# Fewer filler products on TensorE ahead of the last weights of a spectral mixer

## Chip, cores and metric

The kernel runs on one core of a Trainium2 chip. The metric is device time in microseconds (us), the median over several executions. Times are compared with executions of the kernel before on the same chip in the same job, and where a comparison goes across jobs the text says so. The span of a profile (first to last instruction) is about 2.3 us shorter than the device time of the same execution.

TensorE is called PE below, VectorE DVE, ScalarE ACT, GpSimd POOL. PSUM is the memory in which PE's products are summed. A weight *lands* when the DMA transfer that loads it is complete. The *granted clock* is the share of PE's full clock that the profile records.

## The reference, cut to what matters

```python
attn = linear_attention(q, k, v)                  # 8 x 8 heads x 576 x 64, elu + 1 features
x = attn.transpose(0, 2, 1, 3).reshape(8, 576, 512)
X = np.fft.rfft(x, axis=1)                        # the first 64 modes are used
Yr = einsum('bmd,mde->bme', Xr, w_r) - einsum('bmd,mde->bme', Xi, w_i)
Yi = einsum('bmd,mde->bme', Xr, w_i) + einsum('bmd,mde->bme', Xi, w_r)
y = np.fft.irfft(Yr + 1j * Yi, n=576, axis=1)     # other modes are zero
u = x + y
out = u + np.maximum(u @ w_ch, 0.0)
```

Each of the 64 modes has two weights of 512 x 512, `w_r` and `w_i`. Together that is 128 loads which the kernel casts to bf16 while loading, and they fill most of the time (55.7% of the span on the chain of waits of the kernel before).

## The kernel before

The modes are computed in the order in which their weights land. Every mode is two groups of four concurrent products (`t = 1` with `wr`, `t = 0` with `wi`), an eviction from PSUM (by DVE for even modes, ACT for odd ones), and four small products that gather the result (`yt`). By the timeline of before such a group of four takes 0.47 us at full clock, where three fillers in a row, of as many columns each, take 0.82. The last mode, 63, is computed in a turned form, 16 columns wide, so that no eviction and gathering follow it: one copy puts it into `YT`. In the last four modes the kernel adds *fillers*: products whose result nobody reads, meant to keep PE's clock up. The code is shortened; comments stand for what is left out.

```python
def keep_warm(n):
    for _ in range(n):                         # 128 rows, 512 columns, result overwritten later
        pin(nc.tensor.matmul(last_ps[0], id16, wch16[:, 0, :]))

def mode_product(kk, ps, stage, yt_ps):
    wr, wi = w_get(kk)
    # ... st: the evicted mode; P: a PSUM bank
    for t, w in ((1, wr), (0, wi)):
        for dc in range(NDC):                  # NDC = 4 concurrent products, 32 columns of the array each
            mm = nc.tensor.matmul(P[0][dc * 32 : dc * 32 + 32, :], xt_cols(dc, t, kk), w[:, dc, :],
                                  start=(t == 1), stop=(t == 0), tile_position=(0, dc * 32))
        if t == 1 and kk >= NM - 4:
            keep_warm(6)                       # between wr and wi
    if NM - 4 <= kk < NM - 1:
        keep_warm(3)                           # during the eviction
    # ... evict P to st (DVE or ACT), four products yt <- pick_sb, st
    if NM - 4 <= kk < NM - 1:
        keep_warm(3)                           # before the next mode

def last_mode(ps):                             # kk = NM - 1 = 63
    wr, wi = w_get(kk)
    # ... product(t, w, dcs): for each dc four products of 16 columns into y_last
    product(1, wr, range(NDC))
    keep_warm(3)
    product(0, wi, range(3))                   # wi of mode 63 is loaded in two parts
    product(0, wi, range(3, NDC))
    nc.vector.tensor_copy(out=YT[:, :, kk, :], in_=y_last)
```

After the copy into `YT` come eight products `zl <- wch, YT` and four transposes `ypl`, two copies into `last`, and then the output stage: for 36 row tiles the inverse transform and the channel product are summed in PSUM (`acc`), rectified by ACT, added to `x` by DVE and stored.

Of the kernel before, what the change touches and what calls it, by code (L numbers as in the profile page):

```python
# [47 lines left out]
def kernel(  # L48
# [48 lines left out]
    def xt_cols(dc: int, t: int, kk: int):  # L97

        c0 = dc * XDC + t * B * NM + kk
        return xt_c[:, c0 : c0 + 31 * NM + 1 : NM]  # L100
# [231 lines left out]
    def w_get(kk: int):  # L332
        if kk not in w_in:
            w_in[kk] = [w_load(kk, half, wpool, "w", W_KEEP) for half in range(2)]
        return w_in.pop(kk)

    def keep_warm(n: int):

        for _ in range(n):
            pin(nc.tensor.matmul(last_ps[0], id16, wch16[:, 0, :]))  # L340

    def mode_product(kk: int, ps, stage, yt_ps):

        wr, wi = w_get(kk)
        st = stage.tile([128, D], F16, tag="ystage", bufs=2, name=f"ys{kk}")

        n_part = 1
        pw = D // n_part
        P = [
            ps.tile([128, D], F32, tag="P", bufs=2, name=f"P{kk}_{i}")[:, 0:pw] for i in range(n_part)  # L350
        ]
        for t, w in ((1, wr), (0, wi)):
            for i in range(n_part):
                for dc in range(NDC):
                    mm = nc.tensor.matmul(  # L355
                        P[i][dc * 32 : dc * 32 + 32, :], xt_cols(dc, t, kk),
                        w[:, dc, i * pw : i * pw + pw],
                        start=(t == 1), stop=(t == 0), tile_position=(0, dc * 32),
                    )
                    if kk >= NM - 4:  # L360
                        pin(mm)
            if t == 1 and kk >= NM - 4:
                keep_warm(6)
        if NM - 4 <= kk < NM - 1:
            keep_warm(3)
        for i in range(n_part):
            dst = st[:, i * pw : i * pw + pw]
            if (kk + i) % 2 == 0:
                nc.vector.tensor_copy(out=dst, in_=P[i])  # L369
            else:  # L370
                nc.scalar.copy(out=dst, in_=P[i])  # L371
        for ec in range(NDC):
            mm = nc.tensor.matmul(  # L373
                yt_ps[:, ec, kk % 8, :], st[:, ec * 128 : ec * 128 + 128], pick_sb
            )
            if kk >= NM - 4:
                pin(mm)
        if NM - 4 <= kk < NM - 1:
            keep_warm(3)

    def last_mode(ps):

        kk = NM - 1
        wr, wi = w_get(kk)
        y_last = ps.tile([128, NDC, 2 * B], F32, tag="P", bufs=2, name="y_last")

        def product(t, w, dcs):
            for dc in dcs:
                c0 = dc * XDC + t * B * NM + kk
                x = xt_c[:, c0 : c0 + (2 * B - 1) * NM + 1 : NM]  # L390
                for ec in range(NDC):
                    pin(
                        nc.tensor.matmul(
                            y_last[:, ec, :], w[:, dc, ec * 128 : ec * 128 + 128], x,
                            start=(t == 1 and dc == 0 and ec == 0), stop=(t == 0 and dc == NDC - 1),
                            skip_group_check=True,
                        )
                    )

        product(1, wr, range(NDC))  # L400
        keep_warm(3)
        product(0, wi, range(3))
        product(0, wi, range(3, NDC))
        nc.vector.tensor_copy(out=YT[:, :, kk, :], in_=y_last)
# [23 lines left out]
    def mode(kk: int):  # L428
        nonlocal yt_ps
        if kk % 8 == 0:  # L430
            yt_ps = psW.tile([128, NDC, 8, 2 * B], F32, tag="yt", bufs=1, name=f"yt{kk // 8}")
        if kk == NM - 1:
            last_mode(psW)
            return
        mode_product(kk, psW, ystage, yt_ps)
        if kk == NM - 2:
            nc.vector.tensor_copy(out=YT[:, :, NE : NM - 1, :], in_=yt_ps[:, :, 0 : NL - 1, :])
        elif kk % 8 == 7:
            nc.vector.tensor_copy(out=YT[:, :, kk - 7 : kk + 1, :], in_=yt_ps)
# [299 lines left out]
```

## Time and profile before

| | before |
|---|---|
| device time, median of 3 | 432.05 us (431.16 to 432.51) |
| span of the profile | 429.8 us |
| weights | stream at about 214 GB/s to about 390 us |
| last landing of a weight (DMA records) | 394.50 us |
| start of the last copy into `YT` | 395.68 us |
| from there to the end of the span | 34.1 us |

First the page's slices of the kernel before: PE's busy share and its granted clock, each in tenths, in 40 slices of 10.7 us.

```profile
PE   0358776887018776856886666778675758999993
PEclk9999666565558765566556678555658655999998
```

(The first 9s of the clock lie before the first record of it.) In most of the span PE alternates between half and full clock; only slices 34 to 38, counted from 0, from 365 us on, run at full clock throughout, and PE is busy in nearly all of that time.

Next the chain of waits of the kernel before, at its last modes. Columns are start, duration, engine and work.

```profile
...
386.66 1.40 PE zl L340 x6
388.06 0.40 PE P L355 x3
...
394.05 0.47 PE y_last L393 x16
394.52 0.65 PE zl L340 x3
395.17 0.49 PE y_last L393 x16
...
395.68 0.23 DVE YT L404
...
395.97 1.06 PE zl L674 x8
...
397.62 1.03 PE acc L549 x4
...
```

`zl L340` are the fillers: they stand on the chain itself. Nothing in this stretch waits for a DMA: between 382 and 396 us the view of PE's waits has one line (total in us, times, longest).

```profile
PE zl L674 <- DVE YT L404: 0.3, 1, 0.3
```

Now four stretches of the same profile that coincide with the 3.41 us steps of its clock records. Columns are the stretch, its length, the busy time of PE, PEld (weight loads), DVE, ACT and POOL with the number of instructions, the granted clock, the DMA share and GB/s.

```profile
384.69:388.10 3.41, 3.36 (x24) 1.20 (x22) 0.59 (x1) 0.00 (x0) 0.00 (x0) 1.00 1.05 211
388.10:391.52 3.42, 3.42 (x23) 1.27 (x24) 0.00 (x0) 0.58 (x1) 0.00 (x0) 1.00 0.92 179
391.52:394.93 3.41, 3.36 (x35) 1.56 (x34) 1.31 (x2) 0.00 (x0) 0.00 (x0) 1.00 0.26 47
394.93:398.34 3.41, 2.71 (x34) 1.97 (x32) 0.65 (x2) 1.26 (x3) 0.19 (x1) 1.00 0.00 0
```

PE is busy nearly all the time in the first three, for 2.71 of 3.41 us in the fourth, and the clock is 1.00 in all four. The output stage of the same kernel, in the same columns, is PE's as well: it is busy in every moment of 19.3 us.

```profile
402.70:422.00 19.30, 19.30 (x98) 8.91 (x98) 17.14 (x14) 15.53 (x30) 0.00 (x0) 1.00 0.91 364
```

### The profile page before, as it was taken

The page shows a single profiled execution, that of the slowest core. Times are in us where ns is not written, and L with a number is a line of the kernel's source. Part 1 is how long each engine was busy: PE and PEld are TensorE (multiplying, and loading weights), DVE is VectorE, ACT ScalarE, POOL GpSimd, SP SyncE. Part 2 cuts the span into 40 slices and gives each one's busy share as a digit, 9 for nine tenths or more (in the row PEclk, how much of TensorE's full clock was granted, in tenths as well). Part 3 has the DMA queues.
Part 4 walks back from the last instruction along what each step waited for, and adds up shares of the span by engine and source line. Part 5 has one row for each costly group of instructions (what it writes and reads, how often), then busy time and mean ns, then how long its engine had stood idle before and what let it go on. Part 6 is the DMA issues. An engine that isn't in the chain of part 4 may idle for free.

```text
span 429.8 us, 6238 instructions
## 1 busy us (share of the span) xinstructions
PE 296.9 (69%) x2551; PEld 154.8 (36%) x2551; DVE 181.9 (42%) x373; ACT 146.6 (34%) x227; POOL 91.5 (21%) x165
## 2 busy tenths in 40 slices
PE   0358776887018776856886666778675758999993
PEld 0346555664003332322232222322222324954441
DVE  1699998955004233233232322332323322211694
ACT  3687666631002222222222322122212222311782
POOL 4232223222102312121112221221211121110200
PEclk9999666565558765566556678555658655999998
DMA  8999999999999999999999999999999999995697
GB/s 148 207 208 209 209 210 210 211 214 215 222 211 214 215 213 214 214 214 214 213 213 214 214 213 214 213 214 214 213 213 214 214 214 214 214 213 97 239 369 296
DMA packets 35803, 92.38 MB, mean 215 GB/s; under 512 B 3136, under 2 KB 16448, under 8 KB 35776
## 3 DMA queue, kind: packets, MB, share of 16 engines
q0 software_dynamic: 32000, 82.00, 98.2%
q1 hardware_dynamic: 3776, 10.00, 6.1%
q8 instruction: 20, 0.33, 0.3%
q14 instruction: 7, 0.06, 0.0%
HBM read 164.07 MB, written 9.44 MB: 404 GB/s over the span
## 4 chain that ended last, share of the span: by engine, by line
DMA 67%; PE 17%; issue 7%; DVE 4%; ACT 2%; POOL 1%; DVEq 0%; POOLq 0%; ACTq 0%
DMA wi<-in_moe_w_i_dram 33%; DMA wr<-in_moe_w_r_dram 22%; DMA k<-in_k_dram 11%; PE acc L549 4%; PE P L355 3%; PE z L530 2%; PE zl L340 2%; PE acc L593 2%; PE eps L507 2%; PE yp L534 1%; DVE x L272 1%; ACT ke L187 1%; DVE k L194 0%; ACT qT L223 0%; POOL q L169 0%
## 5 line engine op out<-in xcount | busy, mean ns | idle before, releaser
L507 PE MATMUL eps<-wch,xTw 128*128 128x512 f16 x144 | 62.3, 582 | 3.4 <-DVE xTw L504 3.1
L515 ACT CAST E<-eps 128x512 f16<-128x512 f32 (+1 forms) x40 | 21.3, 543 | 122.7 <-PE eps L507 122.7
L115 POOL DMA_DIRECT2D wr<-in_moe_w_r_dram x64 | 34.0, 531 | 135.5 <-PE P L355 109.4
L355 PE MATMUL P<-wi,xt_c 128*32 128x512 bf16 x252 | 42.1, 565 | 27.3 <-DMA wi<-in_moe_w_i_dram 27.3
L355 PE MATMUL P<-wr,xt_c 128*32 128x512 bf16 x252 | 42.6, 582 | 22.9 <-DMA wr<-in_moe_w_r_dram 20.9
L115 POOL DMA_DIRECT2D wi<-in_moe_w_i_dram x65 | 34.5, 531 | 108.5 <-PE P L355 74.1
L355 PEld LDWEIGHTS <-xt_c 128*32 128x32 bf16 x504 | 24.3, 163 | 67.8 <-issue 38.7
L369 DVE CAST ys<-P 128x512 f16<-128x512 f32 x32 | 22.0, 688 | 59.7 <-PE P L355 59.7
L151 PEld LDWEIGHTS <-qT 64*128 64x128 f16 (+1 forms) x640 | 21.5, 126 | 56.8 <-issue 41.8
L371 ACT CAST ys<-P 128x512 f16<-128x512 f32 x31 | 18.1, 585 | 63.2 <-PE P L355 63.0
L373 PE MATMUL yt<-pick_sb,ys 128*128 128x16 f16 x252 | 16.8, 177 | 31.6 <-DMA pick_sb<-row_pick 20.4
L504 DVE COPY xTw<-xTp 128x512 f16<-128x512 f16 x36 | 15.2, 423 | 51.8 <-PE xTp L502 51.8
L373 PEld LDWEIGHTS <-ys 128*128 128x128 f16 x252 | 12.3, 105 | 51.1 <-issue 23.4
L151 PE MATMUL num<-kv,qT 64*128 64x65 f16 (+1 forms) x320 | 14.0, 230 | 22.6 <-ACT kv L247 20.1
L507 PEld LDWEIGHTS <-xTw 128*128 128x128 f16 x144 | 14.7, 124 | 33.7 <-issue 24.2
L492 DVE TENSOR_TENSOR x_main<-nw,rd 128x256 f32<-128x256 f32 x32 | 12.1, 419 | 33.8 <-PE nw L151 33.7
L187 ACT ACTIVATE qe<-q 128x1152 f16<-128x1152 f16 x16 | 17.7, 1155 | 22.9 <-DMA q<-in_q_dram 22.9
L216 PE MATMUL qTp<-id,qe 128*128 128x128 f16 x144 | 16.6, 310 | 12.1 <-DVE qe L200 11.7
L499 ACT CAST x16w<-x_main 128x512 f16<-128x512 f32 x32 | 19.8, 619 | 14.2 <-DVE x_main L492 14.2
L272 DVE TENSOR_TENSOR x<-num,rd 128x512 f16<-128x512 f32 x32 | 22.1, 691 | 1.1
L491 DVE RECIPROCAL rdw<-nw 128x4 f32<-128x4 f32 (+1 forms) x40 | 5.5, 170 | 38.3 <-PE nw L151 38.2
L502 PE MATMUL xTp<-id,x16w 128*128 128x128 f16 x144 | 19.4, 278 | 2.8 <-ACT x16w L499 2.4
(71 smaller groups left out, 413.7 us busy)
## 6 DMA issues: line engine op xcount, KB each, us to landing
wr<-in_moe_w_r_dram POOLq DMA_DIRECT2D x64, 512.0 KB, 18.6
wi<-in_moe_w_i_dram POOLq DMA_DIRECT2D x63, 512.0 KB, 18.6
out_dram<-x_main SPq DMA_DIRECT2D x14, 512.0 KB, 3.1
q<-in_q_dram POOLq DMA_DIRECT2D x8, 576.0 KB, 13.5
k<-in_k_dram POOLq DMA_DIRECT2D x8, 576.0 KB, 14.7
v<-in_v_dram POOLq DMA_DIRECT2D x8, 576.0 KB, 16.9
out_dram<-x_main SPq DMA_DIRECT2D x4, 256.0 KB, 3.4
out_dram<-x_tail SPq DMA_DIRECT2D x2, 512.0 KB, 3.4
```

Source lines behind the costliest of these rows:

```text
L115: tc.keep_in_program_order(nc.gpsimd.dma_start(out=w[:, dcs], in_=rows_of[:, dcs, :]))
L151: mm = nc.tensor.matmul(num[hpo][orow, c0 : c0 + 65], qT[rows, hpp, h2, cols], kv_sb[rows, hpp, h2, :])
L187: pin(nc.scalar.activation(out=ev[:, c], in_=heads(nm, b)[:, c], func=AF.Exp))
L272: nc.vector.tensor_tensor(out=dst.rearrange("p (o c d) -> p o c d", o=2, c=4), in0=nv[:, :, :, 0:64], in1=rden.unsqueeze(3).broadcast_to([ ...
L355: mm = nc.tensor.matmul(P[i][dc * 32 : dc * 32 + 32, :], xt_cols(dc, t, kk), w[:, dc, i * pw : i * pw + pw], start=(t == 1), stop=(t == 0) ...
L369: nc.vector.tensor_copy(out=dst, in_=P[i])
L371: nc.scalar.copy(out=dst, in_=P[i])
L373: mm = nc.tensor.matmul(yt_ps[:, ec, kk % 8, :], st[:, ec * 128 : ec * 128 + 128], pick_sb)
L499: nc.scalar.copy(out=x16, in_=x)
L502: nc.tensor.transpose(xT_ps[:, c, :], x16[:, c * 128 : c * 128 + 128], id16)
L507: nc.tensor.matmul(e_ps, xT[:, c, :], wch16[:, c, :], start=(c == 0), stop=(c == NDC - 1))
L515: nc.scalar.copy(out=dst, in_=e_ps[:, cols])
```

## The change

The intent was to take fillers away where they delay PE. There were 39; 20 are left. `FILL[kk]` gives the numbers between `wr` and `wi`, during the eviction, and before the next mode. The diff is shortened.

```diff
             if t == 1 and kk >= NM - 4:
-                keep_warm(6)
+                keep_warm(FILL[kk][0])
         if NM - 4 <= kk < NM - 1:
-            keep_warm(3)
+            keep_warm(FILL[kk][1])
 # ... eviction and yt products
         if NM - 4 <= kk < NM - 1:
-            keep_warm(3)
+            keep_warm(FILL[kk][2])
+
+    FILL = {60: (2, 1, 1), 61: (4, 2, 2), 62: (4, 2, 1), 63: (1, 0, 0)}
 # ... last_mode
         product(1, wr, range(NDC))
-        keep_warm(3)
+        keep_warm(FILL[kk][0])
         product(0, wi, range(3))
```

Nothing else changes its order on any engine. (The line numbers of later code move by two: L674 of before is L676 after.)

## The prediction

> **What bounds the kernel now.** Median 432.05 us; profiled span 429.8. The page's slices show DMA at 90% or more until slice 36 (weights, about 214 GB/s); the chain of waits is 67% DMA, but only up to 360 us. Then PE is behind (timeline): YZ rows to 379, two accumulators to 382.3, then modes 60 to 63 with 39 fillers to 395.7, all on the chain. From 397.6 to 422 PE is 95 to 100% busy at full clock (stretch table).
>
> **What the change removes.** Fillers go 12 to 4, 12 to 8, 12 to 7 and 3 to 1: 19 of 39, spaced 0.217 us, so 4.1 us of PE work on the chain. The rest keeps its order; the weight DMAs were all issued by 380.8, before the first filler, so they don't move.
>
> **How much is critical.** Landings before (DMA records): wr62 387.1, wi62 389.55, wr63 392.0, the two parts of wi63 393.85 and 394.5. PE used them at 390.06, 391.86, 393.89 and 395.01, so never waited, with 0.5 us of slack at the end. Laid out with before's durations (product 0.41, its end to yt about 0.8, yt 0.11):
> - wr61 at 384.9, wi61 386.3, wr62 388.1: PE-limited.
> - wi62 meets its landing (389.6); wr63 waits to 392.05; wi63 to 393.9, its last quarter to 394.55.
> - The last copy into YT starts near 395.05 in place of 395.68.
>
> So 0.6 (0.5 to 0.8) of 4.1 us is gained; the rest becomes PE waiting for DMA.
>
> **The clock.** [...] the trace's clock records agree (1.0 or 0.5, in steps of 3.41 us). I added up streamed columns per window, as a share of it. Full-clock windows up to about 0.38 were followed by half, from 0.38 by full; half-clock windows needed 0.66 or more to go up. Before, the last windows have 0.73 and more, and 0.59 at 394.9. In the changed kernel, windows starting between about 388.6 and 393.4 would have 0.13 to 0.35 (a y_last product streams 16 columns, a filler 512). That range is longer than a window, so whatever the phase one is too idle: chance of a drop 85% (estimate). Full clock returns after a dense window, at 397.8 to 401.2. Half clock from 395.1 to there costs 1.3 to 2.9 us; the PE-bound output stage can't win it back.
>
> Sum: -0.6, and +1.2 to +2.7 with a drop. Predicted 433.2 us, 8 in 10 between 430.8 and 435.0. Chances: faster by over 2% 0.01, within 2% 0.98, slower 0.01.
>
> **What the profile would show.**
> - 20 fillers (L340); landings unmoved within 0.5 us.
> - PE waits for DMA wr/wi between 389 and 394.6; the chain's DMA part ends at wi63's landing.
> - y_last's copy at 394.8 to 395.2.
> - Clock 0.5 for one or two windows within 392 to 401; zl products from YT at 0.4 us or more in place of 0.27. Once full again, the output stage takes before's time.
> - Last accumulation at 423 to 425 in place of 422.
>
> **What would make it wrong.** [...] If the tail re-warms at once, about even. If the clock falls already in modes 61 to 62, or re-warming takes longer, 435 or more. If landings move, so does the 0.6.

Two passages are cut out of it: a premise about what sets the clock, and a condition built on that premise. 432.05 - 0.6, and 1.2 to 2.7 more with a fall of the clock, is 432.7 to 434.2 us, and about 431.4 without a fall. "The clock" rests on the trace of before: its clock records (only 1.0 and 0.5, in steps of 3.41 us) and its products. The sums per window, their limits of 0.38 and 0.66, the moment at which full clock returns and the cost of 1.3 to 2.9 us are my estimates from that trace; how the sums are scaled stands below, above their table.

## The result, and the profile after

The changed kernel took 432.62 us (median of 4, 432.27 to 433.06) against 431.69 us of the kernel before (4 executions). The ratio is 1.002, with a 95% interval of 0.9999 to 1.0042. A repetition below (e1) shows that it is truly slower, by 0.43%.

The slices after, as above:

```profile
PE   0358677797028776777687677677787858976993
PEclk9999866655558866555856558556555568997998
```

PE's share in slices 35 and 36 (376 to 398 us) falls from 9 to 7 and 6 tenths, and in slice 36 the clock has a 7 where before had a 9. The chain of waits shows the same stretch:

```profile
...
378.14 15.67 DMA wi<-in_moe_w_i_dram
...
393.86 0.30 PE y_last L395 x4
...
394.19 0.24 DVE YT L406
...
394.47 1.90 PE zl L676 x8
...
396.97 1.77 PE acc L551 x4
...
```

The fillers have left the chain. In their place stands the load of the last weight, landed at 393.82; the last four products follow 0.04 us later and the copy into `YT` starts 0.37 us after the landing (before: 1.18 us after it). That is the gain. The loss comes next: the eight `zl` products take 1.90 us, not 1.06, and the four `acc` products 1.77 us, not 1.03, together 1.6 us more. The durations agree with the clock records: the median `zl` product takes 273 ns where they say full clock and 421 ns where they say half. Two lines from the view of the tile `zl` (shortest, median and longest duration in ns), the first of before, the second of after:

```profile
L674 PE MATMUL zl<-wch,YT x8: 272/273/283, 396.0 to 396.7; 128*128 128x256 f16 x8
```

```profile
L676 PE MATMUL zl<-wch,YT x8: 394/421/421, 394.5 to 395.9; 128*128 128x256 f16 x8
```

PE's waits in the changed kernel, from 380 us on (total, times, longest):

```profile
PE P L355 <- DMA wi<-in_moe_w_i_dram: 1.3, 2, 1.0
PE y_last L395 <- DMA wi<-in_moe_w_i_dram: 0.8, 1, 0.8
PE yt L373 <- DVE ys L369: 0.7, 2, 0.5
PE y_last L395 <- DMA wr<-in_moe_w_r_dram: 0.7, 1, 0.7
PE P L355 <- DMA wr<-in_moe_w_r_dram: 0.6, 1, 0.6
...
```

These are 3.4 us of waiting for weights (1.3 + 0.8 + 0.7 + 0.6), where the kernel before had none; the longest single wait is 1.04 us. The removed fillers were 4.1 us (19 at 0.217 us), so most of them turned into waits. And the stretches of the clock, in the columns used before:

```profile
384.86:388.28 3.42, 2.25 (x15) 0.83 (x15) 0.00 (x0) 0.27 (x1) 0.00 (x0) 1.00 1.05 211
388.28:391.69 3.41, 1.81 (x22) 0.79 (x22) 1.32 (x2) 0.00 (x0) 0.00 (x0) 1.00 0.93 180
391.69:395.10 3.41, 2.17 (x32) 1.27 (x29) 0.22 (x1) 0.00 (x0) 0.00 (x0) 0.50 0.18 33
395.10:398.51 3.41, 3.23 (x14) 1.71 (x13) 0.42 (x1) 1.87 (x4) 0.81 (x2) 0.50 0.00 0
402.70:422.00 19.30, 19.22 (x97) 8.90 (x96) 17.15 (x14) 15.53 (x31) 0.00 (x0) 1.00 0.92 367
```

A window in which PE was busy for 1.81 of 3.41 us was followed by half clock for two windows. From 398.5 on the clock is full again and the output stage is as before. What it lost in those windows it never wins back.

The sum over the whole tail is simple. In the kernel before, 34.1 us pass from the start of the copy into `YT` to the end of the span; in the changed kernel 35.8 us (430.0 - 394.19). The copy starts earlier, but 1.7 us more follow it.

### The profile page after: what moved, and what is told of

Read it like the earlier page. It is cut to its first block, busy times and chain, and to the rows that moved or that the text cites. A ratio compares the mean times of both kernels' runs of the same rounds, so it can differ in the third digit from the quotient of the medians.

```text
span 430.0 us, 6200 instructions
## 1 busy us (share of the span) xinstructions
PE 296.6 (69%) x2532; PEld 153.6 (36%) x2532; DVE 181.8 (42%) x373; ACT 146.8 (34%) x227; POOL 91.5 (21%) x165
## 4 chain that ended last, share of the span: by engine, by line
DMA 67%; PE 13%; issue 8%; DVE 8%; POOL 2%; ACT 1%; DVEq 0%; POOLq 0%; ACTq 0%
DMA wi<-in_moe_w_i_dram 37%; DMA wr<-in_moe_w_r_dram 22%; DMA k<-in_k_dram 7%; PE acc L551 4%; DVE x L272 3%; PE P L355 2%; PE z L532 2%; PE acc L595 2%; PE eps L509 1%; PE yp L536 1%; DVE qe L200 1%; DVE q L194 1%; DVE rd L269 1%; DVE k L194 1%; DVE ke L200 1%
## 5 line engine op out<-in xcount | busy, mean ns | idle before, releaser
L355 PE MATMUL P<-wi,xt_c 128*32 128x512 bf16 x252 | 43.1, 573 | 26.6 <-DMA wi<-in_moe_w_i_dram 26.5
L494 DVE TENSOR_TENSOR x_main<-nw,rd 128x256 f32<-128x256 f32 x32 | 12.1, 420 | 34.2 <-PE nw L151 34.2
```

Source lines behind the costliest of these rows:

```text
L355: mm = nc.tensor.matmul(P[i][dc * 32 : dc * 32 + 32, :], xt_cols(dc, t, kk), w[:, dc, i * pw : i * pw + pw], start=(t == 1), stop=(t == 0) ...
```

## The experiments

Theory A: the fillers were on PE's chain, but the landing of the last weight caps the gain at about 0.6 us; the idle time so made lets the clock fall, which costs 1 to 3 us. Rival B: the clock does not matter at the end; the fillers just became waits for DMA.

| run | median | before in the same job | ratio (95%) | copy into `YT` starts | from there to the end | clock after 384 us |
|---|---|---|---|---|---|---|
| e1 changed kernel again | 433.14 | 431.27 | 1.0043 (1.0028 to 1.0058) | 394.40 | 36.5 | half, 393.2 to 400.0 |
| e2 fillers in the waits | 430.85 | 431.27 | 0.9992 (0.9977 to 1.0007) | 394.26 | 34.0 | full |
| e3 fillers of 32 rows | 438.77 | 431.27 | 1.0176 (1.0154 to 1.0197) | 400.81 | 35.5 | half, 387.2 to 404.3 |
| e4 no fillers | 432.51 | 431.27 | 1.0027 (1.0014 to 1.0039) | 394.12 | 36.1 | half, 386.3 to 400.0 |
| e5 before, no last load | 431.81 | 431.85 | 0.9994 (0.9977 to 1.0011) | 394.85 | 34.0 | full |
| e6 changed, no last load | 428.88 | 431.85 | 0.9935 (0.9918 to 0.9952) | 392.13 | 34.3 | full |
| e7 more fillers in mode 63 alone | 431.26 | 431.85 | 0.9984 (0.9968 to 1.0000) | 394.95 | 34.2 | full |
| e8 as e6, more fillers in mode 62 | 428.63 | 431.85 | 0.9932 (0.9914 to 0.9950) | 392.05 | 34.1 | full |
| e9 e2 again | 430.85 | 431.54 | 0.9982 (0.9970 to 0.9995) | 395.26 | 33.9 | full |
| e10 e7 again | 430.97 | 431.54 | 0.9984 (0.9970 to 0.9997) | 394.18 | 34.1 | full |

The last three columns are of the one profiled execution of each. "Full" is to the end of the last accumulation or beyond it. The column "from there to the end" is the span less the copy's start: 33.9 to 34.3 us wherever the clock stays full, 35.5 to 36.5 wherever it does not.

### e1: the changed kernel again

No edit. 

> The changed kernel once more, to get its difference clear of noise. Theory A (at most 0.6 us gained because the last weight landing gates the last mode, then a fall of the granted clock costs 1 to 3 us): 0.3 to 1.8 us slower than before. Rival B (the clock does not matter at the end, the fillers just became waits for DMA): 0 to 0.7 us faster than before.

Measured: 433.14 us, 0.43% over before, with an interval clear of 1. Its mean is 1.9 us above before's, a little more than theory A allowed. Rival B is out by its sign. In the profile the clock is half from 393.16 to 399.99, again two windows, at another phase than in the first profile.

### e2: fillers where PE waits anyway

```diff
-    FILL = {60: (2, 1, 1), 61: (4, 2, 2), 62: (4, 2, 1), 63: (1, 0, 0)}
+    FILL = {60: (2, 1, 1), 61: (4, 2, 2), 62: (4, 3, 4), 63: (5, 0, 0)}
```

> The changed kernel with more fillers only where PE then waits for a weight: mode 62 (4, 3, 4) in place of (4, 2, 1), and 5 in place of 1 in mode 63. They should fit into the waits. Theory A: the copy of the last mode into YT starts within 0.2 us of the landing of the last weight plus 0.35 us, as in the changed kernel, the clock stays at 1.0 to the end, and the time is 0.4 to 0.8 us below before and 1 to 2.5 us below the changed kernel. Rival B: the same as the changed kernel within 0.3 us, since no filler was on the critical path.

Measured: 430.85 us, 2.3 us below the changed kernel of the same job and 0.4 below before, the latter not clear of noise. Its chain of waits:

```profile
...
380.13 13.76 DMA wi<-in_moe_w_i_dram
...
394.26 0.23 DVE YT L406
...
394.54 1.06 PE zl L676 x8
...
396.20 1.03 PE acc L551 x4
...
```

The copy starts 0.37 us after the landing, exactly as in the changed kernel, so the eight added fillers cost nothing. The products behind it take 1.06 and 1.03 us: full clock. PE's position relative to the last landing is the same in both kernels and only the clock differs, so the 2.3 us are the clock's. Rival B falls here.

### e3: the same fillers with a quarter of the rows

In the kernel before:

```diff
-            pin(nc.tensor.matmul(last_ps[0], id16, wch16[:, 0, :]))
+            pin(nc.tensor.matmul(last_ps[0], id16[0:32, :], wch16[0:32, 0, :]))
```

> The kernel before with all its 39 fillers, but each with 32 rows in place of 128: it occupies PE as long (0.217 us), and no DMA wait appears. Theory A, with activity counted by rows: windows from 384 to 395 fall to about 0.25 to 0.3, the clock falls to half between 386 and 395 and the time is 1 to 4 us above before. If the clock does not fall, [...] the time equals before within 0.3 us. Rival B: the same time as before within 0.3 us even if the clock falls.

Measured: 438.77 us, 7.5 above before (four executions). The direction is theory A's; the size is not, I had expected 1 to 4 us. (The 0.25 to 0.3 was my estimate from the sums in the traces, with rows as weights.) While the clock is full a filler of 32 rows takes as long as one of 128: six in a row took 1.47 us here, from 382.07, and 1.47 us in before's profile, from 382.66. The stretches of its profile, in the columns used before:

```profile
383.78:387.20 3.42, 3.37 (x24) 1.22 (x20) 0.69 (x1) 0.00 (x0) 0.00 (x0) 1.00 1.07 216
387.20:390.61 3.41, 3.41 (x15) 0.90 (x14) 0.00 (x0) 0.59 (x1) 0.00 (x0) 0.50 1.04 204
390.61:394.02 3.41, 3.41 (x12) 0.88 (x10) 0.00 (x0) 0.00 (x0) 0.00 (x0) 0.50 0.40 72
394.02:397.44 3.42, 3.42 (x15) 0.90 (x14) 1.27 (x2) 0.00 (x0) 0.00 (x0) 0.50 0.02 5
397.44:400.85 3.41, 3.33 (x37) 1.37 (x35) 0.09 (x2) 0.00 (x0) 0.00 (x0) 0.50 0.00 0
400.85:404.27 3.42, 3.00 (x14) 1.84 (x15) 0.61 (x2) 1.02 (x3) 0.00 (x0) 0.50 0.00 0
```

In the first window PE is busy for 3.37 of 3.42 us, as in the kernel before, and the clock falls all the same; it stays half through further windows in which PE is busy without a pause. So the busy time that a profile shows does not decide the clock by itself. What I had missed in the size: at half clock the fillers themselves take almost twice the time (six of them 2.67 us in the chain, not 1.40), and here they all stand on PE's chain. The copy into `YT` therefore starts at 400.81, 5.1 us later than in before's profile, and the tail behind it is 1.4 us longer (35.5 in place of 34.1).

### e4: no fillers

```diff
+    FILL = {60: (0, 0, 0), 61: (0, 0, 0), 62: (0, 0, 0), 63: (0, 0, 0)}
```

> No fillers at all. Theory A: the copy into YT is gated by the same last landing, so nothing more is gained than in the changed kernel; the clock falls earlier (from about 386 to 392) and comes back no earlier than 398, so the time is equal to the changed kernel or up to 2 us above it, 0.5 to 3.5 us above before. Rival B: equal to the changed kernel within 0.3 us and not above before.

Measured: 432.51 us, 1.2 above before and 0.6 below the changed kernel of that job, where I had expected equal or above. PE's waits from 379 us on:

```profile
PE P L355 <- DMA wi<-in_moe_w_i_dram: 2.5, 2, 1.8
...
PE y_last L395 <- DMA wi<-in_moe_w_i_dram: 1.2, 1, 1.2
PE P L355 <- DMA wr<-in_moe_w_r_dram: 1.0, 1, 1.0
...
```

The copy starts 0.37 us after the landing (393.75) once more. With no filler at all PE gains nothing over the changed kernel, it only waits longer. The clock falls at 386.3, two windows earlier than in e1, which costs nothing because PE is waiting there; it comes back at the same moment, 400.0, after the window from 396.6, which the dense products behind the copy fill. So the 20 fillers of the changed kernel bought nothing: they were too few, or in the wrong places, to hold the clock, which e2 holds with 28 and e7 below with 24. Why e4 is even 0.6 us faster than e1 is only partly seen: in the two profiles the last landing differs by 0.27 us and the tail by 0.4 us. I leave it open.

### e5 and e6: without the last mode's load

The last mode takes mode 62's weights, so the stream ends one mode (about 5 us) sooner. The result is wrong (one of 64 modes; the difference stayed within the tolerance of the comparison). The same edit is made in the kernel before (e5) and the changed kernel (e6); the lines in which mode 62 keeps its weights are left out here.

```diff
         kk = NM - 1
-        wr, wi = w_get(kk)
+        wr, wi = w_last.pop()        # kept by mode 62
```

> The kernel before, but mode 63 is not loaded: it uses the weights of mode 62 (wrong result on purpose), so the weight stream ends 5 us earlier. Theory A says that the kernel before is limited by PE and its fillers here, not by the last landing: no more than 0.4 us faster than before. If instead the last landing gates the kernel before as well, it is 1 to 3 us faster.

> The changed kernel without the load of mode 63 (wrong result on purpose). Theory A: the last landing is what caps the gain of the removed fillers, so the copy into YT now starts 2.0 to 2.7 us earlier than in the changed kernel (near 392) and the time is 1.5 to 3 us below the changed kernel; the clock may still fall (windows of about 0.3 to 0.4). If the removed fillers had not been on the chain, it would equal the run of the kernel before without that load.

Measured: e5 431.81 us against 431.85 of before. Ending the stream earlier gives the kernel before nothing, so its last modes were limited by PE with its fillers. e6: 428.88 us, 3.0 below before and 2.9 below e5. e5 and e6 differ in the 19 fillers alone, so with the last landing out of the way the removed fillers do pay, and the end of e6's chain shows why:

```profile
...
390.43 0.26 PE yt L375 x4
390.69 0.23 PE zl L341
390.92 0.48 PE y_last L397 x16
391.40 0.22 PE zl L341
391.62 0.49 PE y_last L397 x16
...
```

PE goes through mode 63 without a wait, and the copy starts at 392.13, 2.7 us before e5's 394.85, and 2.1 to 2.3 us before those of the changed kernel (394.19 and 394.40, in other jobs). It is not free of landings even so: its chain begins with that of mode 62's `wi`, at 389.13. In e6's profile the clock did not fall; it has no waits for mode 63. That is also why the distance to the changed kernel is larger than the 1.5 to 3 us I had expected: the two were not in one job, but their ratios to before, 0.9935 and 1.0043, are 1.1% or some 4.7 us apart.

### e7: more fillers in mode 63 alone

```diff
-    FILL = {60: (2, 1, 1), 61: (4, 2, 2), 62: (4, 2, 1), 63: (1, 0, 0)}
+    FILL = {60: (2, 1, 1), 61: (4, 2, 2), 62: (4, 2, 1), 63: (5, 0, 0)}
```

> The changed kernel with 5 fillers in place of 1 in mode 63 alone (before the last landings), modes 60 to 62 as changed. Theory A: only windows that end before these fillers, or hold few of them, can still be too idle, so the clock falls in some executions and not in others, by the phase of the window: single times spread between those of the filled version (430.7 to 431.9) and of the changed kernel (433.0 to 433.8), mean 0.3 to 2 us below the changed kernel. Rival B: equal to the changed kernel.

Measured: 431.26 us, single times 430.65 to 431.48. All five lie at the level of e2 (430.67 to 431.86, in another job), none at that of the changed kernel: a miss, I had expected the clock to fall in some executions. The profiled one kept it. By this, four more fillers, between `wr` and `wi` of mode 63, are enough.

### e8: e6 with the clock guarded

`62: (4, 3, 2)` in e6 (wrong result, too). 

> As the changed kernel without the load of mode 63 (wrong result on purpose), with fillers (4, 3, 2) in mode 62 so that no window falls under 0.4. Theory A: clock 1.0 to the end and the copy into YT near 392, so 2 to 3 us below the version with fillers in the waits (that is 2.3 to 3.5 us below before), and 0 to 2 us below the changed kernel without the load.

Measured: 428.63 us, copy at 392.05, full clock. It equals e6 within 0.3 us, as it should if e6 held its clock as well. It is 2.6 us below e7 of the same job, about as far as their copies into `YT` are apart in the profiles (394.95 - 392.05 = 2.9 us).

### e9 and e10: e2 and e7 again

No edit. 

> The version with fillers in the waits once more, to see whether its 0.4 us below before (not clear of noise) repeats. Theory A: 0.2 to 0.9 us below before, the clock at 1.0 from about 364 to 425, no full-clock window under 0.40 after 365. If the earlier difference was noise: within 0.2 us of before.

> The version with 5 fillers in mode 63 alone once more, beside it. Before it was 0.6 us below before, without the falls of the clock in some executions that I had expected. Theory A with the threshold near 0.37: some phase of the window should still catch too little, so one or two of five executions at 432.5 or above; if none falls again, the few fillers at the end are enough in practice and it equals the other version within 0.4 us.

(The 0.37 was my estimate from the sums in the traces; the table in the next section shows no sharp limit.)

Measured: 430.85 and 430.97 us against 431.54: ratios 0.9982 and 0.9984, both intervals below 1. The two versions equal each other, both beat the kernel before by 0.16 to 0.18% in this job, and again no execution of e10 reached the 432.5 us that I had expected of a fall. In their three jobs the 20 executions of the two versions lie between 430.60 and 431.86 us; the 9 of the changed kernel, in two jobs, between 432.27 and 433.81. They do not overlap, which fits a fall of the clock in every execution of the changed kernel. It does not show it: the clock was seen in two of the nine, and single executions of the kernel before, too, reach 432.97.

## Why the prediction was right

**The cap by the last landing: right.** The prediction held that 0.6 (0.5 to 0.8) of the 4.1 us of fillers would be gained. Measured from the landing, the copy moved from +1.18 to +0.37 us, by 0.8. What that is worth when the clock holds, e2, e7, e9 and e10 show: by medians they are 0.4 to 0.7 us below the kernel before of the same job. e5 and e6 show both sides of the cap: the kernel before gains nothing when the last landing is gone, the changed one starts its copy 2.1 to 2.3 us earlier.

**The fall of the clock: right.** Two windows of half clock, 391.7 to 398.5 in the first profile and 393.2 to 400.0 in e1, within the predicted 392 to 401 but for 0.3 us; `zl` products of 0.42 us in place of 0.27; a cost of 1.7 and 2.4 us in the tail, against the predicted 1.3 to 2.9. The clock records of all twelve traces hold only 1.0 and 0.5, in steps that are multiples of 3.41 us (but for a trace's last record); a window below is one such step.

**The time.** 433.2 us was predicted, 432.62 and 433.14 measured. The clock fell in both profiled executions, and the times of the other seven go with a fall; that fits the estimate of 85% and cannot test it closely.

**What was off.** The landings did move, by 0.7 us in the first profile: 393.75 to 394.89 is their range over the traces that load all modes, and the last weight was issued at 378.1 to 381.5 us. That is drift between executions, not the change: in e2 and e9, the same kernel, the last landings lie 1.0 us apart (393.89 and 394.89). For the same reason the last accumulation ended at 422.2, not at 423 to 425: the whole tail began 1.5 us earlier in that profile than in before's. And the limit at "about 0.38" was too sharp. Summing the columns that PE streamed, for every window from 100 us on in all twelve traces, gives the table below. The sum is an estimate: a share of 8192 columns (16 products of 512) at full clock and of half as many at half. The scale is from before's trace, in which equal products of 512 columns in a row start 0.216 us apart at full clock and 0.426 us apart at half (medians), so that 15.8 and 8.0 of them fit into 3.41 us. Each product is counted in the window in which it starts, concurrent 32-column products are counted a quarter, and all are weighted by their share of 128 rows.

| sum, as a share of the window | full-clock windows | followed by half clock |
|---|---|---|
| under 0.25 | 90 | 90 |
| 0.25 to 0.40 | 71 | 34 |
| 0.40 and over | 226 | 1 (at 420.7 us, where PE's work ends) |

Of the half-clock windows none of 395 under 0.55 was followed by full clock, all of 20 over 0.85 were, and 105 of the 349 between. (If products on a border are shared out between the windows, some windows change their row: then 96 of 96, 26 of 54 and 3 of 237.) This sum is my own, worked out from the records; that a sum of this kind fits is shown, that the hardware forms exactly it is not. e3 shows that the rows belong in it: its window at 383.8 has 0.82 without them and 0.26 with them, and the clock fell. The window before the fall in the changed kernel has 0.28 (0.23 in e1), within the predicted 0.13 to 0.35; with e10's four more fillers the lowest window late in the modes is 0.44.

## What to carry to other kernels

In this kernel a filler cost nothing only where PE would wait anyway: find the landing or eviction that ends each wait, and put in as many as fit before it. Taking fillers off the chain helped here until the next releaser, the last landing; beyond that it bought waiting time (3.4 us of waits for 4.1 us of fillers) and the clock fell just before the densest stage, though no wait was longer than 1.04 us; two windows at half clock cost this kernel about 2 us (1.7 and 2.4 in the two profiles). When a stage seems to end in a fixed offset from one event (about 34 us after the copy, as long as the clock was full), check that offset in each experiment first: it tells a later start from a slower run.
